# First layer of the expert blocks with the weights stationary and its output transposed in place

## The chip, the cores and the metric

The kernel runs on one core of a Trainium2 chip. A core has a matrix engine (TensorE, PE in the profile), three engines for elementwise work (VectorE or DVE, ScalarE or ACT, GpSimd or POOL), an engine that mostly issues transfers (SyncE or SP), and 16 DMA engines between the chip's memory and the on-chip memory. TensorE holds a stationary operand, loaded by an LDWEIGHTS instruction (PEld in the profile), and streams a moving operand of some columns past it. The metric is the device time of one execution in microseconds; lower is better.

## The reference

Attention with a memory term makes x (2304 tokens of 512). A top-1 mixture of 8 experts maps x to x, and a soft mixture of experts with 32 slots makes the output. The change lies in the top-1 mixture:

```python
logits = x @ w_gate + modality_bias[modality_id]
e_idx = np.argmax(logits, axis=1)
...
gate_w = probs[np.arange(N), e_idx]
for e in range(E):                       # 8 experts
    mask = e_idx == e
    h = np.maximum(x[mask] @ w1[e], 0.0)          # 512 -> 1024
    out[mask] = gate_w[mask, None] * (h @ w2[e])  # 1024 -> 512
```

## The kernel before

Three stages follow one another: attention (to about 258 us), the top-1 expert blocks (about 286 to 556 us) and the soft mixture (to the end). Routing sorts the tokens of each expert into blocks of 128 tokens; here 18 are computed. Block 0 has code of its own (`first_x`, `first_g1`, ...); block b from 1 to 17 is one call of `body(b)`, and the blocks from 15 on lie inside branches (`from_`, L1498 and after), since the number of blocks depends on the data.

The work on a block b is spread over several bodies, so that PE finds work while others prepare:

- `xc(b)` scales the gathered tokens and splits them into two f16 parts, hi (ACT, L991) and lo (DVE, L992), side by side in `x16`; SP then issues a DMA transpose (L994) into `xT`, which has hidden units on the partitions and the 128 tokens on columns: four 128x128 pieces of hi and four of lo. It stands two bodies ahead of its use.
- `g1(b, f)` is the first layer's half f (512 of its 1024 outputs). Weights too are in two f16 parts, w1h and w1l. `terms` (L1001) issues the products hi*w1h, hi*w1l and lo*w1h: for each of four k, three matmuls with a 128x128 piece of xT stationary and 512 columns of w1h or w1l moving, all into one PSUM bank: 12 matmuls per half, 24 per block, 408 in 17 blocks. Then ACT writes relu as hi (L1015) and DVE the rest as lo (L1016) into `hs`, tokens on partitions.
- SP issues a DMA transpose per half (L1017) from `hs` to `hts`, 34 in all, since the second layer needs the hidden units on partitions.
- `g2(b, f)` is the second layer: again `terms`, pieces of hts stationary, 512 columns of w2h and w2l moving. `y(b)` scales by the gate (ACT, L1029).

`body(b)` issues g1(b), then SP's weight prefetches and xc(b + 2), then g2(b - 1). Small functions passed as `fill` put matmuls of the soft mixture's logits (m2a, m2b, m2c; L1034, L1042, L1050) between the groups of g1. Blocks 9 and 13 take up tokens of small leftover groups (`small1`, `small2`, L1303), whose weights come into `va` over SP (L1293); from body 12 on ACT's queue loads va for the last stage (L906). `prefetch` (L1261 to L1267) reads a table `tab` into registers (L960) and, where the next block begins a new expert, loads its 2 MB of w1 into `rw1` or w2 into `rw2` (L1264); both pass SP's queue, in the order of the program.

The tiles are taken from rings by `rot`: x16, xT, h16 (in hs) and hT (in hts) have two places each. The order of each engine's instructions is that of the code (a manual schedule); waits between engines are semaphores set by the program's dependencies. Late in the last bodies `lvs` lists tiles that are free by then and take up pieces of the last stage's weights; xt, hs and hts are among them.

Of the kernel before, what the change touches and what calls it, by code (L numbers as in the profile page):

```python
# [28 lines left out]
def make_consts(nc, const):  # L29
# [9 lines left out]
    # keys on partitions, queries on columns: queries before the key are masked  # L39
# [5 lines left out]
    # the same for the two 64-row tails that share a chunk; the other side's keys are masked out  # L45
# [5 lines left out]
    # queries on partitions, keys on columns  # L51
# [15 lines left out]
def emit_attention(tc, cs, x_all, q, k, v, M_prev, z_prev, beta, ps_m, ps_s, junk, once, at):  # L67
    nc = tc.nc
    ctx = ExitStack()
    with ctx:  # L70
# [17 lines left out]
        # masked scores of which only the maximum counts  # L88
# [23 lines left out]
        def fills():  # L112
            nc.gpsimd.memset(x_all[0:64, 0, :], 0.0)
            # rows 66 and up meet zeros of the queries' side
            for t in qs2:
                nc.vector.memset(t[:, :, 64:128], 0.0)
            for t in k2s:
                nc.vector.memset(t[64:128], 1.0)
            for t in vhs:
                nc.gpsimd.memset(t[:, :, 64:65], 1.0)  # L120
            for t in vls:
                nc.gpsimd.memset(t[:, :, 64:65], 0.0)
# [81 lines left out]
        def tr1(p):  # L204
            """keys and queries of pair p, and phi of the pair before"""
            a, b = 18 if p == NP else 0, 18 if p == 0 else 27
            nc.sync.dma_start_transpose(out=tts[p % NTT][:, a:b, :], in_=flat(srcs[p % NSRC][:, a:b, :]))
# [7 lines left out]
        def max_mm(j, part):  # L215
            """scores of the high parts, queries on partitions"""
# [20 lines left out]
        def max_red(j, part):  # L237
# [18 lines left out]
            else:  # L256
                # goes on from the tails' own keys
# [55 lines left out]
        def av(j, c):  # L313
# [4 lines left out]
            # both sides' tails share the even side's bank  # L318
# [28 lines left out]
        def mem_mm(j):  # L347
            """phi(q) M and phi(q) z of head j; the odd side brings both tails"""
# [24 lines left out]
        def mem_x(j):  # L373
            """x <- g * (phi(q) M) / (phi(q) z + 1e-6)"""
# [6 lines left out]
        def banks(j):  # L381
            """the odd side brings both tails, which are in the even side's bank"""
            return [(st["av", j], 0, 4)] + ([(st["av", j - 1], 4, 1)] if j % 2 else [])
# [10 lines left out]
        def norm(j):  # L394
            """x += (1 - g) * (e v) / (sum e + 1e-9)"""
# [38 lines left out]
# columns of the places: blocks of 128 tokens, and of up to 32  # L434
# [12 lines left out]
class Route:  # L447
    """top-1 gating of the tokens and their places in the experts' regions of xs"""

    def __init__(self, tc, keep, pool, wk, cs, x_all, xs, mod_id, w_gate, mod_bias):  # L450
# [3 lines left out]
        # gate weights, padded to a column tile  # L454
# [3 lines left out]
        # modality of each token, in units of 64  # L458
# [15 lines left out]
        # iota constants  # L474
# [6 lines left out]
        # token = 64 (iot[p, t] - 1) + p  # L481
# [16 lines left out]
        # tri[k, p] = 1 where k < p  # L498
# [10 lines left out]
        # of the small blocks: experts, and whether there are so many; rows of xs of the two groups of four  # L509
# [3 lines left out]
        # lower[p, e, e'] = 1 where e' < e  # L513
# [36 lines left out]
    # gate logits of nine tiles, 128 columns of x at a time: acc[32 g + e, 128 i + p] of tile 3 g + i  # L550
# [50 lines left out]
    def r4(self, half):  # L601
        """the first of the largest, and its probability"""
# [20 lines left out]
    def r5(self, half, ps):  # L623
        """rank in the expert: tokens of earlier tiles, and of earlier rows of the tile; and the counts"""
# [36 lines left out]
    def r8(self, half):  # L661
        """place[p, t, i] = 1 where row p of tile t has place i in its block"""
# [5 lines left out]
    def store(self, half, c0, c1, sides=range(2)):  # L668
        """columns of x in the order of the tokens"""
# [6 lines left out]
    def r9(self):  # L676
        """the expert with most tokens so far goes first; the others follow it in order"""
# [20 lines left out]
        # its first block is full: of nine tiles' tokens it has an eighth or more  # L698
# [31 lines left out]
    def tables(self, cp, ps):  # L730
        """per block b (partition of tab): expert, valid, first of its expert, next expert, whether there is one.
        gidx[p, b]: the row of xs at place p of block b, out of bounds where there is none; pad[p, b] 1 there."""
# [14 lines left out]
        def by_expert():  # L747
            # a rest of up to 32 tokens is a small block; the first expert has two blocks
# [22 lines left out]
        def by_token():  # L771
            # column of each token, and from it the rows of each block
# [19 lines left out]
        def rows():  # L792
# [6 lines left out]
            # 64 and more; none: 0  # L799
# [56 lines left out]
class Moe2Consts:  # L856
    def __init__(self, nc, const, cs, phi2):
# [5 lines left out]
        # sel[32 g + s, s'] = (s == s')  # L863
# [5 lines left out]
        # sele[r][32 g + s, 32 g' + s'] = (s == s') where s is a slot of expert 4 r + g, -2^15 times for the upper two g'  # L869
# [12 lines left out]
class Stream:  # L882
    """The soft experts' weights in 32 pieces of 1 MB, in the order of their use.
    Pieces 8 q + 4 i + g: i-th half of matrix q % 2 of expert 4 (q // 2) + g, in rows, the last eight in columns."""
# [5 lines left out]
    def load(self, i, tile, eng=None, h=None):  # L890
        """the piece, or its half h; a pair of tiles takes the halves"""
# [16 lines left out]
    def row(self, i, k, f):  # L908
        """row k of the two"""
# [4 lines left out]
def emit_moe(tc, cs, rt, w1_half, phi2, rw1, xb0, xs, cbuf, w1, w2, v1, v2, out, xctx, pctx, ps_m):  # L914
# [5 lines left out]
    with ctx:  # L920
# [7 lines left out]
        # rows of two blocks and their transposes; the hidden layer's; and its transposes  # L928
        xt = fp.tile([128, 4, 8, 128], F16, name="xt")
        hs = fp.tile([128, 2, 16, 128], F16, name="hs")  # L930
# [3 lines left out]
        lvs += [t.rearrange("p i k f -> p (i k f)").bitcast(F32) for t in (xt, hs)]  # L934
# [4 lines left out]
        with ExitStack() as cx:  # L939
# [3 lines left out]
            def rot(tag, n, shape=None, dt=F32):  # L943
                """the next of n tiles that take turns"""
# [8 lines left out]
            for tag, i, t in (("x16", 0, xt), ("xT", 2, xt), ("h16", 0, hs), ("hT", 0, hts)):  # L953
                ring[tag], turn[tag] = [t[:, i], t[:, i + 1]], 0
# [7 lines left out]
            def split(raw, hi, lo):  # L962
                """WS times the weights in two parts"""
# [22 lines left out]
            def xc(b):  # L986
                """the block's rows, in two parts, transposed; and their gates"""
                xb = xbs[b % 2][:, 0:XW]
                x16, xT = rot("x16", 2), rot("xT", 2)
# [7 lines left out]
            def terms(ps, a, i, wh, wl, start, stop):  # L997
                """ps += a w, without the product of the low parts"""
# [4 lines left out]
            def g1(b, f, fill=()):  # L1003
                xT = st["x", b]
                ps = rot("ps_g", 4)
                sl = slice(512 * f, 512 * f + 512)
                for k in range(4):
                    terms(ps, xT, k, w1h[:, k, sl], w1l[:, k, sl], k == 0, k == 3)
                    if k < len(fill):
                        fill[k]()  # L1010
                if f == 0:
                    st["h", b], st["hT", b] = rot("h16", 2), rot("hT", 2)
                h, hT = (st[i, b][:, 8 * f:8 * f + 8] for i in ("h", "hT"))
                hi, lo = flat(h[:, 0:4]), flat(h[:, 4:8])
                nc.scalar.activation(out=hi, in_=ps, func=AF.Relu)  # L1015
                nc.vector.scalar_tensor_tensor(lo, ps, 0.0, hi, op0=ALU.max, op1=ALU.subtract)  # L1016
                nc.sync.dma_start_transpose(out=hT, in_=flat(h))  # L1017
# [29 lines left out]
            def m2c(s, neg):  # L1047
                """logits of the soft experts for the block's tokens, and their softmax over the slots"""
# [20 lines left out]
            def gm(n):  # L1069
                """soft-expert inputs of n blocks' tokens, with the running maximum of each slot"""  # L1070
# [46 lines left out]
            # block 0, of the weights as they come  # L1117
# [32 lines left out]
            def first_split(c, f):  # L1150
                """as split, between ScalarE and GpSimd"""
# [6 lines left out]
            def first_xc():  # L1158
                """block 1's rows"""
# [8 lines left out]
            with tc.manual_schedule():  # L1168
                # not before the rows of block 0
# [46 lines left out]
                st["x", 1] = rot("xT", 2)  # L1216
# [10 lines left out]
            # two pieces in space that the end of the kernel takes  # L1227
# [3 lines left out]
            # buffers in the order of the pieces  # L1231
# [10 lines left out]
            # blocks of a group of four, and the last  # L1242
# [16 lines left out]
            def prefetch(b, i):  # L1259
                """matrix i of the expert that follows the one whose first block is b, or pieces of the soft experts"""  # L1260
# [13 lines left out]
            # small blocks in groups of four experts, 32 tokens of each, in the weights as they come  # L1274
# [9 lines left out]
            def small_load(g, i, ps):  # L1284
                """pieces of matrix i: half p // 4 of its rows of the group's expert p % 4"""
# [48 lines left out]
            def body(b, end=None, after=None):  # L1334
                """first layer of block b, second layer of the one before, logits of the soft experts of the one before that"""
# [18 lines left out]
                # logits of the small blocks of a group of four, which the bodies 9 and 13 take too  # L1354
# [18 lines left out]
                if b == 1:  # L1373
                    # the first expert has two blocks or more
# [36 lines left out]
            def last(b):  # L1411
                """block b is the last"""
# [11 lines left out]
                # the second layer in halves of the columns  # L1424
# [22 lines left out]
            def final():  # L1447
                """the last block: logits with the slots on partitions, and a column with the maximum so far"""
# [37 lines left out]
                # the sum of the weights, 1 of which is the maximum's column  # L1486
# [9 lines left out]
            def from_(b):  # L1496
                """block b, of which there is one, and those that follow"""
# [25 lines left out]
        # ---- soft experts  # L1523
        with ExitStack() as cx:
# [4 lines left out]
            def refill(h, *pairs):  # L1529
                """halves h of pieces"""  # L1530
# [6 lines left out]
            # the weights of the slots, per token tile  # L1537
# [3 lines left out]
            def first(r, ks):  # L1541
                """first layer's products"""
# [36 lines left out]
            # the transposed weights of the slots, 16 times, as rows [hi, lo, hi, lo], the last two 2^-11 times  # L1579
# [16 lines left out]
            # the columns in two parts  # L1596
            n = 256
            # stores of a part: first token tile, number of them, place in a buffer; the buffers of the parts
# [9 lines left out]
            def sums(j):  # L1608
# [4 lines left out]
                # 16 times the sums: hi, and 2^11 lo, whose sums come -2^15 times  # L1613
# [53 lines left out]
def tile_kernel(ctx, tc, q, k_, v, M_prev, z_prev, beta, mod_id, w_gate, mod_bias, w1, w2, phi2, v1, v2, out, dbg=None):  # L1667
# [3 lines left out]
    # rows of tokens come after 64 that are not used  # L1671
# [51 lines left out]
PERIOD = 10  # L1723
# [117 lines left out]
```

## Time and profile before

| | before |
|---|---|
| time, median of 3 runs | 625.65 us (624.35 to 629.98) |
| profiled execution, span | 622.3 us |
| PE busy | 521.0 us (84%) |
| PE weight loads busy | 295.1 us (47%) |
| DVE busy | 360.8 us (58%) |
| ACT busy | 257.6 us (41%) |
| POOL busy | 223.0 us (36%) |
| DMA queue of SP and ACT (q1) | 102.46 MB, 71.7% of 16 engines' span |

The rows come from the profiled execution, whose span lies 3.35 us below the median of the timed runs. A busy share is the union of an engine's records; matmuls overlap, so the time that one matmul takes from the next is read from the distance of their starts, not from their durations. The granted clock of PE is 1.00 at 2.4 GHz and lower where part of a stretch ran at 1.2 GHz.

### The profile page before, as it was taken

The numbers are of one execution on the slowest core, as the hardware profiler recorded it, in microseconds if no ns is written. First come the engines' busy times: TensorE is split into PE (matmuls) and PEld (weight loads), VectorE is DVE, ScalarE is ACT, GpSimd is POOL, SyncE is SP. The second block draws the span as 40 slices with busy tenths as digits, with TensorE's granted clock in tenths as the row PEclk, the third lists the DMA queues.
The fourth block names the chain that finished last, engine by engine and source line by source line (L and its number), as shares of the span: only waits on it lengthen the run. The fifth ranks groups of instructions, "written<-read, shape, count | busy, mean of one in ns | idle before, by whom it ended". The sixth has DMA issues, their size and how long they took to land. (4 is left out here: it accounts for less than half of the span.)

```text
span 622.3 us, 14762 instructions
## 1 busy us (share of the span) xinstructions
PE 521.0 (84%) x5197; PEld 295.1 (47%) x5197; DVE 360.8 (58%) x1226; ACT 257.6 (41%) x580; POOL 223.0 (36%) x277
## 2 busy tenths in 40 slices
PE   0366898999999999679897979998998969759993
PEld 0145675676767768344443434443443424345342
DVE  5678898999988888688633213535424322422143
ACT  4356667777867656433322111414222212201032
POOL 5155476576666657237912010202121101100000
PEclk9988899999999999989999899998999998977998
DMA  5989698988789894864889888892879996765988
GB/s 119 176 169 172 132 175 171 172 182 179 147 163 171 170 199 83 284 118 110 229 228 207 205 197 237 240 229 55 211 172 235 231 292 154 190 246 200 347 277 278
DMA packets 230408, 120.61 MB, mean 194 GB/s; under 512 B 196166, under 2 KB 210447, under 8 KB 230304
## 3 DMA queue, kind: packets, MB, share of 16 engines
q1 hardware_dynamic: 223520, 102.46, 71.7%
q10 hardware_dynamic: 4288, 11.60, 6.0%
q0 software_dynamic: 2496, 5.32, 3.4%
q8 instruction: 45, 0.74, 0.5%
q14 instruction: 59, 0.48, 0.3%
HBM read 75.93 MB, written 9.91 MB: 138 GB/s over the span
## 5 line engine op out<-in xcount | busy, mean ns | idle before, releaser
L311 POOL TENSOR_TENSOR el<-e 128x512 f16<-128x512 f32 (+2 forms) x128 | 118.9, 953 | 81.4 <-ACT e L305 69.2
L1001 PE MATMUL ps_g<-w1h,xt 128*128 128x512 f16 x272 | 90.9, 384 | 10.8 <-SPq L1364 7.3
L1001 PE MATMUL ps_y<-w2h,hts 128*128 128x512 f16 (+1 forms) x288 | 90.6, 383 | 9.8 <-issue 5.7
L1061 POOL DMA_INDIRECT cbuf<-ce,gidx x17 | 17.7, 1041 | 168.6 <-DVEq L1396 91.4
L338 PE MATMUL avp<-vh,e 128*128 128x65 f16 (+1 forms) x480 | 74.9, 200 | 1.1 <-DVE cfa L388 1.1
L338 PEld LDWEIGHTS <-e 128*128 128x128 bf16 (+1 forms) x960 | 63.7, 103 | 21.2 <-issue 15.2
L305 ACT ACTIVATE e<-sp 128x512 f32<-128x512 f32 (+2 forms) x128 | 61.1, 505 | 30.1 <-PE sp L284 16.5
L338 PE MATMUL avp<-vl,e 128*128 128x65 f16 (+1 forms) x480 | 73.1, 197 | 0.0
L338 PE MATMUL avp<-vl,el 128*128 128x65 f16 (+1 forms) x480 | 72.8, 196 | 0.0
L338 PE MATMUL avp<-vh,el 128*128 128x65 f16 (+1 forms) x480 | 72.5, 196 | 0.0
L1001 PEld LDWEIGHTS <-hts 128*128 128x128 f16 x432 | 43.8, 105 | 53.4 <-issue 9.3
L1001 PEld LDWEIGHTS <-xt 128*128 128x128 f16 x408 | 38.1, 99 | 57.3 <-issue 17.3
L338 PEld LDWEIGHTS <-el 128*128 128x128 f16 (+1 forms) x960 | 62.5, 104 | 0.0
L284 PE MATMUL sp<-q2t,k2t 128*128 128x64 f16 (+4 forms) x288 | 54.3, 246 | 3.8 <-DMA q2t<-qs 3.8
L283 PE MATMUL sp<-tt 128*128 128x64 f16 (+4 forms) x288 | 56.1, 247 | 0.7 <-ACT e L305 0.6
L1001 PE MATMUL ps_y<-w2l,hts 128*128 128x512 f16 (+1 forms) x144 | 55.1, 383 | 0.0
L1015 ACT ACTIVATE hs<-ps_g 128x512 f16<-128x512 f32 x34 | 20.3, 597 | 80.4 <-PE ps_g L1001 70.3
L1001 PE MATMUL ps_g<-w1l,xt 128*128 128x512 f16 x136 | 52.2, 383 | 0.4 <-DVEq L1377 0.4
L378 ACT ACTIVATE x_all<-mmp,cfm 128x64 f32<-128x64 f32 x144 | 32.9, 321 | 28.8 <-DVE cfm L371 17.6
L243 DVE CUSTOM_DVE_ANT_0 mxp<-mxp,mq 128x512 f32<-128x512 f32 (+1 forms) x64 | 39.6, 625 | 7.0 <-PE mxp L229 5.4
L1036 DVE COPY si<-ps 128x512 f32<-128x512 f32 x19 | 13.1, 689 | 51.5 <-PE ps L1034 43.3
L1016 DVE SCALAR_TENSOR_TENSOR hs<-ps_g,hs 128x512 f16<-128x512 f32 x34 | 23.5, 690 | 32.9 <-ACTq L1377 22.3
(412 smaller groups left out, 1128.4 us busy)
## 6 DMA issues: line engine op xcount, KB each, us to landing
va<-in_moe_w_dram SPq DMA_DIRECT2D x12, 1024.0 KB
va<-in_moe_w_dram ACTq DMA_DIRECT2D x9, 1024.0 KB
rw<-in_moe_w_dram SPq DMA_DIRECT2D x8, 1024.0 KB
va<-in_moe_w_dram SPq DMA_DIRECT2D x16, 512.0 KB
raw<-in_q_dram SPq DMA_DIRECT2D x32, 128.0 KB
raw<-in_k_dram SPq DMA_DIRECT2D x32, 128.0 KB
raw<-in_v_dram SPq DMA_DIRECT2D x32, 128.0 KB
rw<-in_moe_w_dram SPq DMA_DIRECT2D x2, 2048.0 KB
```

The lines of the kernel that those rows point to most:

```text
L243: nc.vector.tensor_tensor_reduce(out=ps[:, src:src + n] if out is None else out, in0=ps[:, src:src + n], in1=msk, scale=1.0, scalar=-3.0e3 ...
L283: nc.tensor.matmul(ps[:, dst:dst + n], k1[:, ko:ko + 128], q1[:, qo:qo + n], start=True, stop=False)
L284: nc.tensor.matmul(ps[:, dst:dst + n], k2[:, ko:ko + 128], q2[:, qo:qo + n], start=False, stop=last)
L305: nc.scalar.activation(out=es[j % 2][0][:, a:a + n], in_=st.pop(("sp", j, g))[:, 0:n], func=AF.Exp, scale=0.125)
L311: nc.gpsimd.tensor_tensor(el[:, a:a + n], e[:, a:a + n], hv[:, a:a + n], op=ALU.subtract)
L338: nc.tensor.matmul(dst, l, r, start=(i == 0), stop=(i == len(mms) - 1))
L378: nc.scalar.activation(out=x_all[:, tiles(j, c), 64 * h:64 * h + 64], in_=ps[:, 65 * c:65 * c + 64], func=AF.Copy, scale=cf[:, c:c + 1])
L1001: nc.tensor.matmul(ps, a[:, l, :], r, start=(start and j == 0), stop=(stop and j == 2))
L1015: nc.scalar.activation(out=hi, in_=ps, func=AF.Relu)
L1016: nc.vector.scalar_tensor_tensor(lo, ps, 0.0, hi, op0=ALU.max, op1=ALU.subtract)
L1036: nc.vector.tensor_copy(st["x2t"], tp)
L1061: ins = nc.gpsimd.indirect_dma_start(out=cbuf, out_offset=bass.IndirectOffsetOnAxis(ap=idx, axis=0), in_=ce, in_offset=None, bounds_check= ...
```

## The change

The roles of the two operands of the first layer are exchanged. For each of four groups of 128 outputs, `g1` now issues 12 matmuls with a 128x128 piece of w1h or w1l stationary and the 128 columns of xT (hi or lo) moving, into 128 columns of the same PSUM bank: 48 per half, 96 per block, 1632 in 17 blocks, each with its own LDWEIGHTS. The bank then holds the hidden units on partitions and tokens on columns, as the second layer wants them. ACT and DVE write hi and lo straight into hts, with the same shapes; `hs` and the DMA transposes of L1017 are gone. Its space goes to `xt2`, and the ring of xT has four places instead of two. The products of the sums are the same, in another order. Comments are removed as well, so lines move by one to three.

```diff
-        hs = fp.tile([128, 2, 16, 128], F16, name="hs")
+        xt2 = fp.tile([128, 4, 8, 128], F16, name="xt2")
...
-        lvs += [t.rearrange("p i k f -> p (i k f)").bitcast(F32) for t in (xt, hs)]
+        lvs += [t.rearrange("p i k f -> p (i k f)").bitcast(F32) for t in (xt, xt2)]
...
-            for tag, i, t in (("x16", 0, xt), ("xT", 2, xt), ("h16", 0, hs), ("hT", 0, hts)):
-                ring[tag], turn[tag] = [t[:, i], t[:, i + 1]], 0
+            ring["x16"], turn["x16"] = [xt[:, 0], xt[:, 1]], 0
+            ring["xT"], turn["xT"] = [xt[:, 2], xt[:, 3], xt2[:, 0], xt2[:, 1]], 0
+            ring["hT"], turn["hT"] = [hts[:, 0], hts[:, 1]], 0
...
-                x16, xT = rot("x16", 2), rot("xT", 2)
+                x16, xT = rot("x16", 2), rot("xT", 4)
...
-                sl = slice(512 * f, 512 * f + 512)
-                for k in range(4):
-                    terms(ps, xT, k, w1h[:, k, sl], w1l[:, k, sl], k == 0, k == 3)
-                    if k < len(fill):
-                        fill[k]()
+                for i in range(4):
+                    dst, sl = ps[:, 128 * i:128 * i + 128], slice(512 * f + 128 * i, 512 * f + 128 * i + 128)
+                    mms = [(w[:, k, sl], xT[:, n + k, :]) for k in range(4) for w, n in ((w1h, 0), (w1h, 4), (w1l, 0))]
+                    for j, (l, r) in enumerate(mms):
+                        nc.tensor.matmul(dst, l, r, start=(j == 0), stop=(j == len(mms) - 1))
+                    if i < len(fill):
+                        fill[i]()
...
-                    st["h", b], st["hT", b] = rot("h16", 2), rot("hT", 2)
-                h, hT = (st[i, b][:, 8 * f:8 * f + 8] for i in ("h", "hT"))
-                hi, lo = flat(h[:, 0:4]), flat(h[:, 4:8])
+                    st["hT", b] = rot("hT", 2)
+                hT = st["hT", b][:, 8 * f:8 * f + 8]
+                hi, lo = flat(hT[:, 0:4]), flat(hT[:, 4:8])
...
-                nc.sync.dma_start_transpose(out=hT, in_=flat(h))
```

PE's instructions at the start of the first layer of block 1 (out<-moving and stationary operand; xt stands for xT) were before, a k's three products and the first of the next:

```order
L1001 LDWEIGHTS xt
L1001 MATMUL ps_g_5343<-w1h,xt 128x512
L1001 LDWEIGHTS xt
L1001 MATMUL ps_g_5343<-w1l,xt 128x512
L1001 LDWEIGHTS xt
L1001 MATMUL ps_g_5343<-w1h,xt 128x512
```

and are after the change at the same place:

```order
L1012 LDWEIGHTS w1h
L1012 MATMUL ps_g_5343<-xt,w1h 128x128
L1012 LDWEIGHTS w1h
L1012 MATMUL ps_g_5343<-xt,w1h 128x128
L1012 LDWEIGHTS w1l
L1012 MATMUL ps_g_5343<-xt,w1l 128x128
```

The weights have become the stationary operand, a matmul has 128 columns, and each still has a weight load of its own.

SP's queue at the first bodies, from the transpose of block 2's tokens (xt(2)) to the first prefetch's load of rw1 (rw_93), before:

```order
L994 DMA_TRANSPOSE xt<-xt 128x8x128
L1017 DMA_TRANSPOSE hts<-hs 128x8x128 x2
L960 TENSOR_LOAD tab
L960 ISA x2
L1261 COMPARE_AND_BRANCH
L960 TENSOR_LOAD tab
L960 ISA x2
L1262 COMPARE_AND_BRANCH
L960 TENSOR_LOAD tab
L960 ISA x2
L1264 ISA
L1264 DMA rw_93<-in_moe_w_dram 128x4x1024
```

and after, from the last read of the table to the transpose of block 2's tokens:

```order
L961 TENSOR_LOAD tab
L961 ISA x2
L1267 ISA
L1267 DMA rw_93<-in_moe_w_dram 128x4x1024
L1265 UNCONDITIONAL_BRANCH
L906 DMA rw_93<-in_moe_w_dram 128x4x512 x2
L1265 UNCONDITIONAL_BRANCH
L1264 UNCONDITIONAL_BRANCH
L995 DMA_TRANSPOSE xt_5332<-xt 128x8x128
```

The two transposes of hs are gone, and the transpose of xt(2) has moved behind the load of rw1 (the two loads of L906 belong to the branch that is not taken).

SP's queue behind that, in body 2, from the transposes of hs to the reads for the next prefetch, before:

```order
L1017 DMA_TRANSPOSE hts<-hs 128x8x128
L1377 UNCONDITIONAL_BRANCH
L1017 DMA_TRANSPOSE hts<-hs 128x8x128
L994 DMA_TRANSPOSE xt<-xt 128x8x128
L960 TENSOR_LOAD tab
```

and after:

```order
L1265 UNCONDITIONAL_BRANCH
L1264 UNCONDITIONAL_BRANCH
L1380 UNCONDITIONAL_BRANCH
L995 DMA_TRANSPOSE xt<-xt 128x8x128
L961 TENSOR_LOAD tab
```

Only the transposes of hs have left; the branch and the transpose of the next tokens keep their order.

## Rows read from the trace of the kernel before

**Rows 1.** Busy time by engine in stretches: start:end, length, engines, clock, DMA share, GB/s

```profile
286.00:558.00 272.00, 238.95 (x1337) 111.08 (x1335) 104.34 (x284) 67.86 (x143) 59.80 (x71) 0.94 0.81 206
...
337.00:354.00 17.00, 12.96 (x60) 5.59 (x61) 5.46 (x18) 2.70 (x7) 2.32 (x3) 0.80 0.86 195
```

**Rows 2.** PE's timeline: start, length, line, out<-in, count, idle before and releaser

```profile
293.45 0.38 PE L1001 MATMUL ps_g<-w1h,xt 128*128 128x512 f16 x1 [0.73 <-ACTq L1377]
...
307.72 0.39 PE L1001 MATMUL ps_g<-w1h,xt 128*128 128x512 f16 x1 [2.19 <-DMA xt<-xt]
...
341.04 0.61 PE L1001 MATMUL ps_y<-w2h,hts 128*128 128x512 f16 x1 [4.12 <-DMA hts<-hs]
...
347.10 0.60 PE L1001 MATMUL ps_y<-w2h,hts 128*128 128x512 f16 x2
...
514.52 0.58 PE L1001 MATMUL ps_g<-w1h,xt 128*128 128x512 f16 x1 [7.31 <-SPq L1364]
...
517.78 0.38 PE L1001 MATMUL ps_g<-w1h,xt 128*128 128x512 f16 x1
```

**Rows 3.** PE's waits from 285 us on: line, releaser, total us, times, longest

```profile
PE ps_y L1001 <- issue: 5.7, 1, 5.7
...
PE ps L1443 <- issue: 3.8, 1, 3.8
PE ps_g L1303 <- DMA va<-in_moe_w_dram: 3.2, 1, 3.2
```

**Rows 4.** Costliest groups of the page, the first layer's: count, busy us and mean ns, idle

```profile
L1001 PE MATMUL ps_g<-w1h,xt 128*128 128x512 f16 x272 | 90.9, 384 | 10.8 <-SPq L1364 7.3
...
L1001 PE MATMUL ps_g<-w1l,xt 128*128 128x512 f16 x136 | 52.2, 383 | 0.4 <-DVEq L1377 0.4
```

**Rows 5.** PE's timeline, first of 24 matmuls of a second layer and first after them

```profile
313.95 0.38 PE L1001 MATMUL ps_y<-w2h,hts 128*128 128x512 f16 x1
...
319.13 0.38 PE L1001 MATMUL ps_g<-w1h,xt 128*128 128x512 f16 x1
```

**Rows 6.** PE's timeline in attention, first of eight short pairs and the two matmuls after

```profile
199.93 0.19 PE L338 MATMUL avp<-vh,e 128*128 128x65 f16 x1
...
200.17 0.22 PE L222 MATMUL mxp<-tt 128*128 128x128 f16 x1
200.23 0.27 PE L223 MATMUL mxp<-tt 128*128 128x256 f16 x1
```

**Rows 7.** PE's timeline in the last stage, four transposes of 128 columns and the next

```profile
596.45 0.40 PE L1593 MATMUL ctp<-idh,c 128*128 128x128 f16 x4
596.78 0.64 PE L1574 MATMUL op<-va,hT 128*32 128x256 f32 x8
```

**Rows 8.** Lines L1017 and L1015: count, duration ns min/median/max, first and last start

```profile
L1017 SPq EVENT_SEMAPHORE  x34: 17/17/11015, 287.2 to 533.9; - x34
L1017 SPq DMA_TRANSPOSE hts<-hs x34: 838/1269/5230, 292.8 to 535.4; - x34
...
L1015 ACT ACTIVATE hs<-ps_g x34: 597/597/597, 290.2 to 534.1; 128x512 f16<-128x512 f32 x34
```

**Rows 9.** SP's timeline: start, length of issue, line, transfer, count

```profile
292.76 2.61 SPq L1017 DMA_TRANSPOSE hts<-hs  x2
298.48 0.42 SPq L1264 DMA_DIRECT2D rw<-in_moe_w_dram  x1
299.30 3.73 SPq L994 DMA_TRANSPOSE xt<-xt  x1
...
493.49 1.35 SPq L994 DMA_TRANSPOSE xt<-xt  x1
509.02 5.12 SPq L1017 DMA_TRANSPOSE hts<-hs  x2
```

**Rows 10.** SP's waits from 285 to 560 us, the longest entry

```profile
SPq L1017 <- DMA xt<-xt: 15.6, 3, 11.0
```

**Rows 11.** DVE's timeline, the write of the table

```profile
283.40 0.21 DVE L831 CAST tab<-tT 128x8 int32<-128x8 f32 x1
```

More of the change, by code (lines that the diff above doesn't have):

```diff
@@ L1215, in emit_moe @@
                 first_g2(1, (0, 1))
-                st["x", 1] = rot("xT", 2)
+                st["x", 1] = rot("xT", 4)
                 gate(1)
```

## The prediction

> **What bounds the kernel now.** I read the windows first. From 286 to 558 us, the stretch of the expert blocks, TensorE (PE) is busy 238.95 of 272 us while the DMA engines stand at a mean share of 0.81 [rows 1]; no other engine is near it (DVE 104.34, ACT 67.86). So PE's own instructions set the length of this stretch, plus the 33 us in which it stands still. Then PE's timeline and its waits, to see what ends those pauses. Three of the largest end with something that this change touches: 2.19 us at 307.72 (an xt transpose), 4.12 us at 341.04 (a hts transpose), and 7.31 us at 514.52, where PE waits for SP's passage through the branch at L1364 [rows 2]. The others (3.2 us for a va load, 5.7 and 3.8 us marked "issue") belong to transfers or branches that stay [rows 3]. The first layer is 408 matmuls of 512 columns (272 with w1h, 136 with w1l) [rows 4], all in PE's chain.
>
> **The change, part by part.**
>
> *Matmuls of the first layer: the cost.* Of the 512-column form, 24 (the second layer's, of the same shape) take 319.13 - 313.95 = 5.18 us, 215.8 ns each, and a fresh 128x128 weight load hides in each [rows 5]. Four matmuls of 128 columns replace one, each again with a fresh weight load: 1632 pairs for 408. The columns streamed are the same; the question is what a pair costs when its matmul is short. No long run of 128-column pairs is in this trace, so I bound it.
> Below: attention issues pairs of 65 columns with fresh 128x128 weights, eight between 199.93 and 200.17, 30 ns each, and one of 128 columns from 200.17 to the next start at 200.23, 60 ns [rows 6]. So a weight load by itself holds the next pair for at most 30 ns, and a 128-column matmul should be bound by its columns: a quarter of 215.8, 54 ns, +0.1 us in all. Nothing removes columns, so I see no gain here.
> Above: four 128x128 f16 transposes, each with fresh weights, take 0.33 us from 596.45 to the next line's start at 596.78, 82 ns each [rows 7]: 82 x 1632 - 215.8 x 408 = 133.8 - 88.0 = +45.8 us. That stretch includes a change to another line and to f32.
> I take 57 ns, between 54 and the single reading of 60, which are nearer in kind than transposes ahead of a change of type: 57 x 1632 = 93.0, **+5.0 us**; 60 ns would give +9.9.
> The Trainium skill, "TensorE: Matmul & The Clock Gate", section "Back-to-back issue gap", speaks against the change here: it gives some 81 ns per matmul at N=128 for a stream of weight-load and matmul pairs, an estimate of +44 us. The same section gives 131 ns at N=512, where the rows show 215.8, so its figures do not describe this stream; its formula for a single matmul, N/2.4 + 2.5 or 55.8 ns, would make +3 us.
>
> *The transposes of hs: the gain.* 34 DMA transposes leave SP's queue (median 1.27 us of issue, up to 5.23, with semaphore waits up to 11.0 us) [rows 8], and their transfers leave the rings. ACT's and DVE's evictions keep number, shape and source (34 of 597 ns on ACT [rows 8]); they write hts where they wrote hs, so hts is ready when DVE ends instead of a transfer later. What this buys is only the PE pauses that hung on it:
> - At 341.04 the 4.12 us go. After it 14 of the 512-column matmuls (and a small one) took until 347.10, 6.06 us where 14 take 3.02, in a window with a mean granted clock of 0.80: the engine ran at its lower level, 1.2 GHz, after the pause [rows 1, 2]. With the small one's 0.1 that is 2.9 us more: **-7.0**.
> - At 514.52: SP stood in front of hts(15) until 509.02 because an xt transpose issued at 493.49 had not landed [rows 9]; its longest wait for xt is 11.0 us [rows 10]. Only then did it go on to L1364, for which PE waited. Without the two transposes between, SP passes on, and PE needs only xt(16). The 7.31 us go; eight matmuls from 514.52 to 517.78 took 3.26 us instead of 1.73, 1.5 us more [rows 2]. If 1 us stays as a wait for xt(16) itself: **-7.8**. The other end is nothing, if the branch then waits for ACT's loads of va in the same stretch.
> - The va load at 369.76: 3.2 us [rows 3]. It no longer shares the rings with two hts transposes, but PE also comes earlier. Between -3.2 and +4 (the load lands no sooner while PE arrives 7 us before): I take **-1.5**.
>
> *A moved load: the cost of order.* On SP, xt(2)'s transpose now stands behind the 2 MB load of rw of the first prefetch, where it stood ahead of it. The load needs tab, written at 283.40 [rows 11], and three reads of it; those took from 295.37 (the end of the issue at 292.76) to 298.48, 3.1 us [rows 9]. So it is issued near 286.6, and xt(2) right behind. What a transpose behind that load costs is shown by xt(3): load at 298.48, transpose at 299.30, and PE goes on at 307.72, 9.2 us after the load [rows 2, 9]. So xt(2) is there near 295.8, where PE takes it up at 293.45 now: **+2.4**. Queued behind it are g1(2) and, in PE's order, all that follows. In exchange xt(3) no longer has a load of that size ahead and its 2.19 us at 307.72 go: **-2.2**. The new pause of some 3.3 us may bring the lower clock: none followed 2.19 us, 2.9 us were lost after 4.12; I take **+2**, between nothing and 2.9.
>
> *Rings and late pieces.* xT gets four places instead of two, so a transpose waits for the matmuls of two blocks earlier; xt2 takes hs's place as a late buffer. No pause of PE hung on either. Nothing.
>
> Sum against the profiled execution: 622.3 + 5.0 - 7.0 - 7.8 - 1.5 + 2.4 - 2.2 + 2 = 613.2. The median of the runs shown is 625.65, 3.35 above the profiled span, so **616.6 us** against that median (-1.4%).
>
> **The rivals.**
> 1. *Forecast: the pauses go, a pair takes some 57 ns.* From 608 (pair at 54 ns, -4.9; va's pause gone whole, -1.7; no lower clock at the new pause, -2) to 621.5 (pair at 60 ns, +4.9).
> 2. *Pairs bound by their weights: slower.* PE queues 1632 loads and 1632 matmuls where it had 408 each; at 82 ns [rows 7] the sum is 613.2 + 45.8 - 5.0 + 3.35 = **657**. For it: the row itself. Against it: 30 ns pairs with loads of the same size [rows 6]. The other terms give 14.1 us; they are eaten at (88.0 + 14.1) / 1632 = 62.6 ns per pair, and it is slower by over 1% from 66.4 ns. As 60 is the reading of one pair, that is not far off.
> 3. *The pauses only change their name: same.* At a DMA share of 0.81 [rows 1] the next transfer ends the wait: the va load at 369.76 takes PE's 7 us (+4 for -1.5), or L1364 is held by ACT's loads of va as long as by xt (0 for -7.8). Then **622.1** or **624.4**, with both 629.9. For it: the rings stay filled with weight loads of 1 and 2 MB, which the change leaves. Against it: the 7.31 us ended with SP's own passage, not with a transfer [rows 2].
> 4. *More comes back.* With 34 transposes fewer the pauses marked "issue" (5.7 and 3.8 us [rows 3]) fall to half, -4.7, and xt(2) lands in time, -4.4: **607.5**. For it: both pauses lie in stretches with busy rings. Against it: nothing shows what they wait for.
>
> **Chances.** Forecast 0.58, slow pairs 0.12, renamed pauses 0.16, more gain 0.14. A per cent, 6.3 us, is about what a measurement of this kernel can tell from no change. Faster by over 1% (below 619.4): four fifths of the forecast's case (0.46), all of the fourth (0.14) and a quarter of the third (0.04), 0.64. Within 1%: the rest of the forecast (0.12), most of the third (0.10) and a milder slow pair (0.01), 0.23. Slower: 0.11 of the second and 0.02 of the third, 0.13. The range leaves out the slow pairs, both pauses renamed, and the far edge of the gain: **606 to 629**; the forecast's own is 608 to 621.5.
>
> **What would show it.** PE's timeline: the 12 pairs of a column group should take 0.65 to 0.72 us; at 0.98 (82 ns) the forecast is wrong by 40 us. The pauses at the second layer's start near 341 and at block 16's first layer should be gone; a new one of about 3 us should stand ahead of block 2's first layer near 296, ended by xt, and none of 2 us ahead of block 3's. SP's waits should have no hts in them, and its 11 us wait for xt should be gone. If PE's wait for va near 365 is 7 us or longer, or L1364's counterpart still holds PE for 5 us, the third rival holds. If pair and pauses are as said but the time is not, the pauses in "issue" have grown: PE executes 2448 more instructions.

## The result, and the profile after the change

The changed kernel takes 610.29 us (median of 4 runs, 608.18 to 611.55) against 625.0 us for the kernel before in the same comparison: a ratio of 0.9757, 95% interval 0.9715 to 0.98. The profiled execution has a span of 607.9 us, 14.4 less than before.

The page of the changed kernel, busy time by engine and the queue of SP's and ACT's transfers (packets, MB, share of 16 engines):

```profile
span 607.9 us, 17147 instructions
...
PE 517.0 (85%) x6421; PEld 349.2 (57%) x6421; DVE 360.1 (59%) x1226; ACT 257.7 (42%) x580; POOL 222.7 (37%) x277
...
q1 hardware_dynamic: 187616, 93.55, 65.0%
...
L1012 PEld LDWEIGHTS <-w1h 128*128 128x128 f16 x1088 | 85.4, 99 | 16.1 <-issue 13.0
```

PE is nearly as busy as before in sum (4.0 us less), with 1224 matmuls and as many weight loads more. What has shrunk most, by 10.4 us, is the time in which it stood still. PE's waits from 285 us on, the longest first:

```profile
PE ps_g L1012 <- DMA xt<-xt: 6.6, 1, 6.6
PE ps L1098 <- DVE dg L1086: 3.9, 1, 3.9
PE ps_g L1461 <- issue: 3.8, 1, 3.8
PE ps_y L1002 <- issue: 3.1, 1, 3.1
PE ps L1098 <- DVE al L1084: 1.7, 1, 1.7
PE ps_y L1002 <- ACTq L1416: 1.7, 1, 1.7
```

The 7.3 us for SP's branch, the 4.1 us for hts [rows 2] and the 3.2 us for va [rows 3] are gone. In their place stands one new long pause, 6.6 us for a transpose of xt, and a wait of 1.7 us for ACT near the end. (The waits for DVE at L1098 stood at L1095 before, with 2.1 and 1.7 us.) The stretch of the expert blocks, here taken to 548 us, has a DMA share of 0.64 where it was 0.81 [rows 1] (columns as in that group):

```profile
286.00:548.00 262.00, 236.89 (x2574) 166.80 (x2572) 103.59 (x289) 68.71 (x146) 59.91 (x71) 0.97 0.64 185
...
286.00:303.00 17.00, 10.37 (x131) 9.19 (x130) 10.72 (x36) 5.40 (x10) 12.42 (x13) 0.79 0.75 191
```

PE's timeline around the new pause: the first and the last of 96 pairs of block 1, then block 2, whose first layer waits, two later triples of it, the second layer of block 1, the first layer of block 3, the second layer of block 4 (the one that waited for hts before), and the first layer of block 16 (which waited for SP's branch) with the second layer of block 15:

```profile
288.20 0.28 PE L1012 MATMUL ps_g<-xt,w1h 128*128 128x128 f16 x2
...
293.50 0.22 PE L1012 MATMUL ps_g<-xt,w1l 128*128 128x128 f16 x1
...
300.35 0.37 PE L1012 MATMUL ps_g<-xt,w1h 128*128 128x128 f16 x2 [6.63 <-DMA xt<-xt]
...
300.62 0.42 PE L1012 MATMUL ps_g<-xt,w1h 128*128 128x128 f16 x2
...
300.94 0.42 PE L1012 MATMUL ps_g<-xt,w1h 128*128 128x128 f16 x2
...
309.56 0.38 PE L1002 MATMUL ps_y<-w2h,hts 128*128 128x512 f16 x1
...
314.74 0.28 PE L1012 MATMUL ps_g<-xt,w1h 128*128 128x128 f16 x2
...
344.94 0.38 PE L1002 MATMUL ps_y<-w2h,hts 128*128 128x512 f16 x1
...
504.91 0.28 PE L1012 MATMUL ps_g<-xt,w1h 128*128 128x128 f16 x2
...
511.37 0.38 PE L1002 MATMUL ps_y<-w2h,hts 128*128 128x512 f16 x1
```

Two things are to be read here. The pair of a weight load and a 128-column matmul takes (293.50 - 288.20) / 95 = 55.8 ns. And block 3 follows its predecessor with no pause: 309.56 to 314.74 is 5.18 us, a second layer's 24 matmuls and nothing else, where the kernel before waited 2.19 us for xt(3) [rows 2].

The experiments start block 1 at different times, since attention and routing ahead of it vary by a few us. So beside the timed ratios I use the **tail**: from block 1's first matmul to the end of the span. Before it is 622.3 - 287.37 = 334.9 us (the first matmul of that layer in PE's timeline), after 607.9 - 288.20 = 319.7 us. Marks in the same timelines show where the 15.2 us of the tail come from:

| stretch, from and to | before, us | after, us | difference |
|---|---|---|---|
| first layers of blocks 1 and 2, to second layer of 1 (287.37 to 300.19; 288.20 to 309.56) | 12.8 | 21.4 | +8.5 |
| to first layer of 3 (307.72; 314.74) | 7.5 | 5.2 | -2.4 |
| to second layer of 4 (341.04; 344.94) | 33.3 | 30.2 | -3.1 |
| to second layer of 5 (357.06; 359.42) | 16.0 | 14.5 | -1.5 |
| to second layer of 6, with the small blocks' first part (384.33; 381.19) | 27.3 | 21.8 | -5.5 |
| to second layer of 14 (501.86; 499.73) | 117.5 | 118.5 | +1.0 |
| to second layer of 15 (522.27; 511.37) | 20.4 | 11.6 | -8.8 |
| to the end (622.3; 607.9) | 100.0 | 96.5 | -3.5 |

### The profile page after: what moved, and what is told of

Same layout as the page of the kernel before. It is cut to its first block, busy times and chain, and to the rows that moved or that the text cites. A ratio compares the mean times of both kernels' runs of the same rounds, so it can differ in the third digit from the quotient of the medians.

```text
span 607.9 us, 17147 instructions
## 1 busy us (share of the span) xinstructions
PE 517.0 (85%) x6421; PEld 349.2 (57%) x6421; DVE 360.1 (59%) x1226; ACT 257.7 (42%) x580; POOL 222.7 (37%) x277
## 5 line engine op out<-in xcount | busy, mean ns | idle before, releaser
L311 POOL TENSOR_TENSOR el<-e 128x512 f16<-128x512 f32 (+2 forms) x128 | 118.5, 949 | 82.8 <-ACT e L305 69.1
L1012 PE MATMUL ps_g<-xt,w1h 128*128 128x128 f16 x1088 | 99.5, 222 | 7.5 <-DMA xt<-xt 6.6
L1012 PE MATMUL ps_g<-xt,w1l 128*128 128x128 f16 x544 | 96.0, 222 | 0.0
L1012 PEld LDWEIGHTS <-w1h 128*128 128x128 f16 x1088 | 85.4, 99 | 16.1 <-issue 13.0
L1002 PE MATMUL ps_y<-w2h,hts 128*128 128x512 f16 (+1 forms) x288 | 87.1, 370 | 4.8 <-issue 3.1
L1002 PEld LDWEIGHTS <-hts 128*128 128x128 f16 x432 | 42.5, 102 | 45.9 <-issue 6.1
L1019 ACT ACTIVATE hts<-ps_g 128x512 f16<-128x512 f32 x34 | 20.3, 597 | 87.5 <-PE ps_g L1012 87.5
L1012 PEld LDWEIGHTS <-w1l 128*128 128x128 f16 x544 | 54.1, 99 | 0.0
L1002 PE MATMUL ps_y<-w2l,hts 128*128 128x512 f16 (+1 forms) x144 | 53.4, 371 | 0.0
```

What stands on the lines that cost most here:

```text
L311: nc.gpsimd.tensor_tensor(el[:, a:a + n], e[:, a:a + n], hv[:, a:a + n], op=ALU.subtract)
L1002: nc.tensor.matmul(ps, a[:, l, :], r, start=(start and j == 0), stop=(stop and j == 2))
L1012: nc.tensor.matmul(dst, l, r, start=(j == 0), stop=(j == len(mms) - 1))
```

## The experiments

My theory ahead of them: PE lost time to the transposes in two ways, by waiting for its own hts and because they kept SP's queue and the rings busy; the short pairs cost little; and the new pause comes from SP's order alone. One thing that was said ahead of the prediction was too broad: it is the order of PE, ACT, DVE and POOL that is that of the code; SP's is chosen when the program is built. The code calls `xc(2)` ahead of the first prefetch in both kernels, and still xt(2) came to stand behind the load of rw1 on SP.

| kernel | median, us | ratio to before, 95% interval | span | tail |
|---|---|---|---|---|
| e1_xt2_first | 600.29 | 0.9649 (0.961 to 0.9688) | 598.2 | 310.0 |
| e2_dump | 622.47 | 0.9985 (0.9944 to 1.0025) | 620.0 | 332.7 |
| e3_ring2 | 606.31 | 0.9733 (0.9655 to 0.9812) | 607.1 | 319.3 |
| e4_old_form | 602.23 | 0.9656 (0.9608 to 0.9703) | 604.0 | 317.7 |
| e5_tiny | 610.06 | 0.9762 (0.9634 to 0.989) | 611.0 | 321.1 |
| e6_dump_act | 665.07 | 1.0652 (1.0506 to 1.0798) | 661.8 | |
| e7_after_again | 609.96 | 0.977 (0.9635 to 0.9905) | 610.1 | 320.3 |
| e8_xt2_again | 600.42 | 0.9592 (0.9444 to 0.9739) | 601.2 | 309.3 |

The first four ran on one chip, the last four on another; the kernel before took 623.11 and 626.84 us there.

**e1_xt2_first and e8_xt2_again: undo the order.**

```diff
-                if b == 1:
-
-                    prefetch(0, 0)
                 if nxt:
                     with tc.If(sw[b + 1] > 0):
                         split1(0)
+                if b == 1:
+                    prefetch(0, 0)
```

> The changed kernel with one line moved: body 1 issues the prefetch of rw1 behind the branch that splits weights, so that on SP the transpose of xt(2) stands ahead of that 2 MB load again. Theory (the moved load costs the 6.63 us pause at 300.35 and 2.7 us of lower clock behind it, and pays back 2.2 us at block 3): 610.3 - 9.3 + 2.2 = about 603 us, PE's pause ahead of block 2 under 1 us, a pause of about 2 us ahead of block 3 back. Rival (the transposes and the 2 MB share the rings in any order, the pause only moves to block 3): 609 to 611 us with a pause of 5 us or more at block 3.

> The changed kernel with xt(2) ahead of the load of rw1, again, to take its difference to the changed kernel from one call: 6 to 8 us less.

The first gave 600.29 us, beside 606.31 for e3, which has the order of the changed kernel; the second 600.42 us beside 609.96 for the changed kernel itself (e7). The tails, 310.0 and 309.3 us against 319.7 and 320.3, say 9.7 to 11 us, more than the 6 to 8 that was expected. SP's timeline of e1, then PE's, block 2 and block 3:

```profile
286.78 1.30 SPq L995 DMA_TRANSPOSE xt<-xt  x1
295.71 0.41 SPq L1267 DMA_DIRECT2D rw<-in_moe_w_dram  x1
296.53 9.36 SPq L995 DMA_TRANSPOSE xt<-xt  x2
```

```profile
294.46 0.28 PE L1012 MATMUL ps_g<-xt,w1h 128*128 128x128 f16 x2 [0.73 <-ACTq L1377]
...
306.74 0.27 PE L1012 MATMUL ps_g<-xt,w1h 128*128 128x128 f16 x2
```

xt(2) goes out ahead of the load, which is issued at 295.71, and block 2 starts at 294.46 with the 0.73 us that the kernel before had, too [rows 2]. No pause stands ahead of block 3, neither the rival's 5 us nor the 2 us that the theory expected back, although xt(3) is again issued behind the load (296.53); e8 has none there either. So the price is not just moved along. A pause of 1.95 us in e8 stands ahead of block 2, with no load ahead of its xt(2). SP's timeline of e8, then PE's:

```profile
291.74 1.29 SPq L995 DMA_TRANSPOSE xt<-xt  x1
299.78 0.41 SPq L1267 DMA_DIRECT2D rw<-in_moe_w_dram  x1
```

```profile
299.74 0.27 PE L1012 MATMUL ps_g<-xt,w1h 128*128 128x128 f16 x2 [1.95 <-DMA xt<-xt]
```

By itself, then, xt(2) took 8.0 us from its issue to PE's start. This kernel beats both the kernel before and the changed one.

**e2_dump: the transposes stay, but PE needs nothing that they bring.**

```diff
-            ring["xT"], turn["xT"] = [xt[:, 2], xt[:, 3], xt2[:, 0], xt2[:, 1]], 0
+            ring["xT"], turn["xT"] = [xt[:, 2], xt[:, 3]], 0
+            ring["dump"], turn["dump"] = [xt2[:, j] for j in range(4)], 0
...
                 nc.vector.scalar_tensor_tensor(lo, ps, 0.0, hi, op0=ALU.max, op1=ALU.subtract)
+                nc.sync.dma_start_transpose(out=rot("dump", 4), in_=flat(hT))
```

(and rot("xT", 2) for rot("xT", 4) in both places.)

> The changed kernel with the 34 transposes issued all the same, from hts into a place nobody reads (xT's ring has two places again to make room). SP's order is then that of the kernel before, and nothing on PE waits for what the transposes bring. Theory (part of the gain is PE no longer waiting for its own hts, part is SP's queue and the rings being free): the 4.1 us pause at 341 stays gone, the 7.3 us pause for SP's branch at block 16 and the wait for va come back; about 620 us, 616 to 624. Rival a (only the direct wait for hts mattered): about 606 to 611 us, no pause at block 16. Rival b (all of the gain is SP's queue and the rings; the wait for hts was only a sign of it): 627 to 630 us.

622.47 us, a ratio of 0.9985: all the gain is gone, inside the theory's range and at its upper part. PE's waits:

```profile
PE ps_g L1013 <- SPq L1369: 5.5, 1, 5.5
PE ps_y L1003 <- issue: 5.2, 1, 5.2
...
PE ps_g L1308 <- DMA va<-in_moe_w_dram: 4.3, 2, 2.5
PE ps_g L1013 <- DMA xt<-xt: 3.1, 2, 1.7
...
PE ps_y L1308 <- DMA va<-in_moe_w_dram: 2.5, 1, 2.5
```

The branch at block 16, the va loads (6.8 us in sum) and xt are back; the wait for hts at 341 is not. The two waits for xt stand ahead of block 2 and of block 3:

```profile
294.80 0.27 PE L1013 MATMUL ps_g<-xt,w1h 128*128 128x128 f16 x2 [1.68 <-DMA xt<-xt]
...
308.02 0.27 PE L1013 MATMUL ps_g<-xt,w1h 128*128 128x128 f16 x2 [1.42 <-DMA xt<-xt]
```

SP's own waits name the lane that my prediction named for the kernel before [rows 10]:

```profile
SPq L1022 <- DMA xt<-xt: 22.0, 3, 9.9
```

So most of what the transposes cost was not PE waiting for them. Rival a (606 to 611 us) falls. Rival b (627 to 630) falls as well, if barely: with the short pairs included the kernel should be about 3 us above the kernel before, and is 2.2 us below it in the tail, some 5 us for the wait at 341 and its clock.

**e3_ring2: xT with two places.** The edit is the first pair of lines of e2's, without the ring "dump".

> The changed kernel with xT's ring of two places as before. Theory (the ring brings nothing): 609 to 611.5 us, like the changed kernel. Rival (the deeper ring lets the token transposes be issued earlier, which is where part of the gain comes from): 613 us or more, with new PE waits for xt.

606.31 us; the ratio of 0.9733 and the tail of 319.3 us are those of the changed kernel (0.9757 and 319.7). The time lies below the expected 609 in part because the whole comparison ran lower on that chip (before at 623.11); its interval is 5 us wide to either side. No gain from the deeper ring shows.

**e4_old_form: the old matmuls without transposes.** The edit is to the kernel before. It leaves out the transposition, so the second layer multiplies other numbers.

```diff
-                hi, lo = flat(h[:, 0:4]), flat(h[:, 4:8])
+                hi, lo = flat(hT[:, 0:4]), flat(hT[:, 4:8])
...
-                nc.sync.dma_start_transpose(out=hT, in_=flat(h))
```

> The kernel before with the transposes of hs left out and hi and lo written straight into hts (untransposed, so the second layer multiplies other numbers: the transposition is what is left out). Its first layer keeps the 408 matmuls of 512 columns. Against the ring-of-two kernel it tells what the 1632 short pairs cost. Theory (0.2 us per block, 3 to 4 us in all): 606 to 608 us. Rival (the short pairs are free, or help, since the clock or the weight loads go better): 610 us or more.

602.23 us, 4.1 less than e3 (0.9656 against 0.9733), with the same SP order. The time lies below the expected 606 to 608, as e3's lies below its own. In the tail the difference is 1.6 us (317.7 against 319.3), and by the pitch it is (55.8 x 1632 - 215.8 x 408) / 1000 = 3.0 us. The three agree on a small cost, 1.6 to 4.1 us.

**e5_tiny: SP's entries without their volume.** From e2:

```diff
-                nc.sync.dma_start_transpose(out=rot("dump", 4), in_=flat(hT))
+                nc.sync.dma_start(out=rot("dump", 4)[0:1], in_=hT[0:1])
```

> As the kernel that issues 34 transposes nobody reads, but each transpose replaced by a copy of one partition (2 KB) of hts. SP's queue keeps its 34 entries, their order and their waits for ACT and DVE; the rings lose the volume of the transposes. SP's order has xt(2) ahead of the load of rw1. Theory (the pauses come from the time that the transposes take on the rings, and with it from SP's entries that wait for their lanes): about 600 us, like the kernel with xt(2) first, 598 to 604, no pause of 5 us at block 16. Rival (SP's standing in front of the evictions is what makes its token transposes and va loads late): 612 us or more, with the waits for va and the pause at block 16 as with the transposes.

The changed kernel ran beside it as e7:

> The changed kernel, beside the others on the same chip. 607 to 611 us, with the pause of 6 us ahead of block 2.

It gave 609.96 us.

e5 gave 610.06 us: neither. The 5.5 us for SP's branch and the waits for va are gone, as the theory wants, but the time is 10 us above e1 and e8. PE's longest waits:

```profile
PE ps_g L1013 <- DVEq L1382: 4.5, 1, 4.5
PE ps_y L1003 <- issue: 4.4, 1, 4.4
...
PE ps L1039 <- ACTq L1401: 2.8, 1, 2.8
```

The first is not SP's doing. Line L877 is a copy of 32x8 values on DVE that takes 0.16 us in most of the profiles; DVE's timeline and POOL's show what happened to it here:

```profile
293.33 1.69 DVE L877 COPY sele<-rep 32x8 f32<-32x8 f32 x1
...
295.04 1.76 DVE L877 COPY sele<-rep 32x8 f32<-32x8 f32 x1
```

```profile
293.19 12.43 POOL L1288 MEMSET va<- 128x2048 f32 x7
```

From the moment POOL's memsets of va began, four pairs of DVE's small operations took 1.7 us each, until 300.4, and the evictions behind them came some 6 us late (300.40 here, 292.84 in e1, whose block 1 starts 1.7 us sooner). The same slow copies are in the profiles of e4 and e7, where PE waited for xt(2) at that time anyhow, and not in those of the kernel before, the changed kernel, e1, e2, e3, e6 and e8. In e1 the last of them ended near 292.8, when POOL's memsets began at 292.76. From block 1's first matmul to its second layer e5 takes 20.3 us (289.93 to 310.21) where e1 takes 13.4 (288.20 to 301.56). So of the 11 us between the tails of e5 and e1 some 7 are this coincidence, the pause of 4.5 and a granted clock of 0.74 behind it (301.8 to 310.2) above all. What remains, some 4 us, is what SP's standing entries can have cost; the wait of 2.8 us for ACT near block 16 is the largest part. Against e2 the volume alone is worth 332.7 - 321.1 = 11.6 us, and about 18 without the coincidence. No run shows e5 without it, so this split of queue and volume is an estimate.

**e6_dump_act: the same transposes from ACT's queue.** e2's with `nc.scalar` in place of `nc.sync`, and e1's edit.

> The 34 transposes nobody reads, issued from ACT's queue instead of SP's, with the prefetch of rw1 behind the branch so that xt(2) keeps its place ahead of it. The volume is on the rings, SP's queue is free of them, ACT has to wait for DVE's lo before each. Theory (volume and lanes on the rings): waits for va remain, 612 us or more. Rival (SP's queue): near 600 to 606 us, since ACT is busy only a quarter of the stretch.

665.07 us, far above both. SP's waits tell why:

```profile
SPq L996 <- DMA xt<-hts: 120.2, 18, 14.8
```

In this program SP's token transposes waited 120 us in sum for those of ACT. The Trainium skill, "DMA: Bandwidth & Descriptors", section "DMA Transpose (X-bar)", says that two streams that both transpose have to be serialized, which agrees with this row. The row shows the price of that wait, not what the volume costs. As a test of queue against volume this experiment says nothing, since it added a wait that neither theory had.

## Why the prediction was right, and where its terms were off

The forecast was 616.6 us with a range of 606 to 629; 610.29 lies inside, on its fast side, and the sign and mechanism hold: pauses go, short pairs cost little. But the gain is 14.4 us in the span where the sum had 9.1, and it is partly luck that the total came so near: both the gain from the transposes and the cost of the moved load were sized far too small, and the two errors cancelled in part.

- **Pair of 128 columns: right.** Said 57 ns and +5.0 us; measured 55.8 ns, +3.0 by the pitch and 1.6 to 4.1 by e4. The rival at 82 ns falls, and with it the reading of the transposes' row [rows 7] as a pitch. By the rule of the Trainium skill ("TensorE: Matmul & The Clock Gate", "Back-to-back issue gap", 81 ns at N=128) the kernel would have come out near 656 us, an estimate with 81 ns in my sum. The trace disagrees with that rule, and agrees with the same section's isolated formula, 55.8 ns.
- **Wait for hts at 341: right, but not all of it reached the time.** Said -7.0. The second layer at 344.94 starts without a pause and runs at full pitch, so both the 4.12 and the 2.9 us are gone. But in the table the two stretches around it lose only 4.6 us together: four longer first layers (0.2 us each) lie in them, and PE, earlier now, meets new small waits (0.70 us for DVE the longest). e2, which removes this wait alone, is 2.2 us below the kernel before, 5 with the pairs' cost taken out.
- **Branch at block 16: right.** Said -7.8; the stretch lost 8.8. e2 brings back 5.5 us of it when the transposes are issued though nobody reads them; e5, without the volume, has no wait for SP's branch, but 2.8 us for one of ACT's. That fits the prediction's account, xt(16) landing late with hts behind it in SP's queue; that it landed late for the volume of the transposes, and not for their entries, rests on e5 alone. The wait that I left for xt(16) itself was not there.
- **Wait for va: too small.** Said -1.5; the stretch lost 5.5. The sum feared that PE would arrive earlier and the load would not. SP, freed of hts, issued it earlier too: the last pair of va loads now goes out at 354.31, with 12 us to PE's first matmul on va at 366.03; before it was 360.00 and 363.67. SP's timeline after the change, then PE's after and before it:

```profile
354.31 2.64 SPq L1296 DMA_DIRECT2D va<-in_moe_w_dram  x2
```

```profile
366.03 7.41 PE L1306 MATMUL ps_g<-va,si 128*32 128x512 f32 x64 [0.83 <-issue]
```

```profile
363.67 2.86 PE L1303 MATMUL ps_g<-va,si 128*32 128x512 f32 x20 [0.83 <-issue]
369.76 7.04 PE L1303 MATMUL ps_g<-va,si 128*32 128x512 f32 x44 [3.23 <-DMA va<-in_moe_w_dram]
```

  All 64 matmuls run through in 7.4 us, where before 20 and 44 of them lay at both sides of a 3.23 us pause and took 2.86 and 7.04 us, some 2.5 us more. The granted clock from 369.70 to 377.00 was 0.77, and 1.00 after the change, so a stretch at the lower clock went with the pause. The pause's price was its length and the clock behind it, which the sum had counted at 341 and forgotten here. The third rival, that pauses only change their name, has little support: e2 shows the va pauses to hang on the transposes, and the new waits at 341 and at the end are small.
- **Moved load: right in place, too small by a factor.** Said +2.4 and +2 for the clock, -2.2 at block 3, +2.2 in all; the table has +8.5 and -2.4, and e1 puts the whole at 9.7 us, 8.0 of it in the stretch to the second layer of block 1. The step that failed was to take 9.2 us from load to PE's start from one xt(3). The load went out at 287.96, not 286.6, and PE went on at 300.35, 12.4 us behind it:

```profile
287.96 0.38 SPq L1267 DMA_DIRECT2D rw<-in_moe_w_dram  x1
288.75 25.11 SPq L995 DMA_TRANSPOSE xt<-xt  x3
```

  Then came the lower clock: behind the pause a triple of pairs takes 0.32 us (300.62 to 300.94), where three take 0.17 at the pitch of block 1, and the granted clock from 286 to 303 is 0.79. The 9.2 us from 300.35 to 309.56 would be 6.5 at 2.4 GHz, as 504.91 to 511.37 are for a later block: 2.7 us. From its issue xt(2) took 11.6 us to PE's start here, where xt(3) took 8.4 behind its load [rows 2, 9]. But 7.7 us in e2 (287.07 to 294.80) and 8.0 in e8 are what xt(2) takes with no load ahead, so the prediction's one price from xt(3) held next to nothing for the load. Why a load costs 3 to 4 us here and hardly any ahead of xt(3) stays open; no experiment took the transfers at 288 to 300 apart. The -2.2 came, but not by the exchange under which it was booked: e1 and e8 have the load ahead of xt(3) again and no pause at block 3, while e2, with the transposes, has 1.42 us there. That pause went with the transposes.
- **What the sum left out: the end.** From block 15 on 3.5 us went, 2.6 of it in the pause "issue" of 5.67 us, now 3.10. (The new wait of 1.66 us behind it takes back what the lower clock behind the long pause had cost, 0.60 from 547 to 553 us before; some 0.8 us more lie behind PE's last matmuls.) In e2, with PE's new program and the transposes, it is 5.2 again; in e4, with the old number of instructions and no transposes, 3.6; in e5, with SP's entries but no volume, 4.4. So the longer PE program is not what it hangs on, and less traffic seems to shorten it. That is half of the fourth rival: the other pause in "issue", 3.8 us, stayed at 3.8, and xt(2) did not land in time. What the engine does in it no row names; that it goes with the transposes on SP's queue is shown (5.2 and 5.7 us in the two profiles that have them there, 2.9 to 3.6 in the six without transposes, 3.0 in e6 with ACT's), how is not.

In one balance of tails: e2 to e1 is a gain of 22.7 us for SP's queue and the rings at equal order; the direct wait is a gain of about 5; the short pairs take back about 3 and the moved load 9.7. That makes 15 of the 15.2 us. The chain from before over e2 and e1 to the changed kernel closes by construction; what the runs tell is the shares. The balance of my sum was 16.3 for the pauses and 7.2 for the costs, so a gain of some 28 us stood against 16.3, and a cost of some 13 against 7.2.

## What to carry to other kernels

When a transfer stands in a shared queue, its price is not only the wait that bears its name but what it delays for the others on that queue and on the rings: here 5 us against 23. Take away a transfer, and the program's order on that queue can change elsewhere; print it, and price the new neighbours, as one exchange of two entries cost 10 us and moving one call got them back. A first layer whose output is needed transposed can be had that way from the matmul itself, by exchanging stationary and moving operand, for a few per cent of its matmul time, as long as a fresh weight load hides behind 128 columns.

## What the runs showed of the hardware that I had not expected

- A matmul of 128 columns with its own 128x128 weight load costs 55.8 ns in a long run, although the weight loads are recorded at 99 ns each, so their records overlap.
- Small DVE operations (32x8) took 1.7 us instead of 0.16 us while POOL set 128x2048 values to zero (1.8 us each, 12.43 for seven), in the profiles of e4, e5 and e7; in that of e5 the evictions behind them were some 6 us late.
- SP's DMA transposes waited 120 us in sum for those of ACT's queue in e6: 34 transposes issued from ACT made the kernel 6.5% slower than before, where the same 34 from SP (e2) took the time of before.
- A DMA transpose of one block's tokens with no load ahead of it on SP's queue took 7.7 and 8.0 us from issue to PE's start (e2, e8); behind a load of 2 MB it took 11.6 us once and 8.4 us once.
